# The first steps of a clustered-attention kernel in another order: loads by partition halves, VectorE and GpSimd work moved, and one more maxima row turned on TensorE

## The chip, the cores and the metric

One Trainium2 chip, one of its cores. The metric is the device time of one execution in microseconds (us). Engines are named as in the profile: PE is TensorE (PEld its weight loads), DVE is VectorE, ACT is ScalarE, POOL is GpSimd, SP is SyncE, which only issues DMAs here (SPq in the rows).

## The reference, cut to what matters

Three layers: attention that is masked by clusters, a mixture of eight experts with the best two per token, and a soft mixture. The change lies in the first one.

```python
# q, k, v: 2 batches x 8 heads x 768 x 64; 16 centroids per head
q_assign = np.argmax(np.einsum('bhsd,hcd->bhsc', q_n, c_n), axis=-1)
k_assign = np.argmax(np.einsum('bhsd,hcd->bhsc', k_n, c_n), axis=-1)
mask = q_assign[:, :, :, None] == k_assign[:, :, None, :]
scores = np.where(mask, scale * np.matmul(q, k.transpose(0, 1, 3, 2)), -1000000000.0)
scores = scores - np.max(scores, axis=-1, keepdims=True)
attn = np.exp(scores)
attn = attn / (np.sum(attn, axis=-1, keepdims=True) + 1e-09)
return np.matmul(attn, v)
```

## The kernel before, in words

The 16 heads are worked in 8 pairs. A pair has 12 **steps**: 2 halves of the queries (`qh`) by 6 chunks of 128 keys. The main loop in `body` runs over two steps at a time; pair 0 has steps 0 to 11, pair 1 steps 12 to 23. A **score** (L372 and L374, four products into a `psc` bank) is followed by the exponential on ScalarE (L377, `pt`), and two steps later by `av` (L387, `pav`) on TensorE and the sums of `pt` on GpSimd (L404, L407).

What a pair needs first:

- `load` and `load_s` bring q, k and their stacked form; `sims` multiplies the stacked form with the centroids (L216, `psim`), and DVE turns the result (L219).
- `masks(p, 0..4)` makes one-hot rows of the best cluster: a maximum (L228), an `is_equal` with two SBUF inputs (L230), a transpose (L233), all on DVE; then a product (L237), and two operations on ACT (L238, L241). `mask_rows` carries them into the operands by six DMAs (L281, L285). Pair 0 has its own way: `first_rows` (L250 on PE, L257 on ACT, L261 on DVE).
- `hk`, `hq`, `ak`, `aq` copy the operands on ACT, and `akl`, `aql` make the remainders on POOL (L305, L315), each after the ACT copy it subtracts. POOL also writes constant rows of the operands in `fixed` (L194 to L196).
- The row maxima come ahead of the scores. Per half of the queries there are nine **units** (`munit`): PE multiplies (L333, `pmx`), DVE takes the maximum (L338 and L343, `mp`). Two PSUM banks `mx` take turns, so a unit's product waits for the reduction two units back. `mfin` joins the nine (L348, `nm`) and makes a row of them: for the pairs and halves in `TF` by six small products (L354, `pnm`) and a copy on ACT (L356), for the others by a transpose on DVE (L359, `nmt`) and four DMAs (L362). The scores of that half of the queries need the row.

Every engine does its instructions in the order of the program. That order is written out by hand: before the loop as calls in `body`, and in the loop by the tables `pre` (units, one ahead of each of the two scores, the rest behind them), `mid` (ACT copies) and `post` (everything behind the `av`), with a step for each entry. `U1` and `Z1` set the steps of pair 1's first units and of its first `mfin`, `R1` and `Z0` those of pair 0's second half, `ORD` the mix of `masks(1, ...)` and units ahead of the loop.

`setup2` (L201 to L210) and `Dispatch.setup` (L490 to L516) fill constants for later, nearly all of it on POOL; `Dispatch.setup` has four instructions on DVE, and the first of them (L505, `lim`) waits for POOL (L504). In the kernel before they stand between the first units of pair 0's second half and the loop.

Of the kernel before, what the change touches and what calls it, by code (L numbers as in the profile page):

```python
# [57 lines left out]
B1 = 9  # L58
B7 = 8
B2 = 1  # L60
TF = (0, 0), (0, 1)
RATE = 2, 1, 1, 1, 2, 3, 1, 2, 1, 1, 4, 1, 3
ORD, U1, Z1, R1, Z0 = (1, 1, 1, 0, 1, 0, 1, 1), 3, 8, 4, 2
M2S = 14, 15, 16, 18, 20
MS = 10, 10, 12, 14, 18
G0, GN, KS = 55, 3, 64
# [15 lines left out]
f32 = lambda t: t.bitcast(F32)  # L82


class Attention:
# [6 lines left out]
    def __init__(self, tc, g, qk, q2, k2, v2, cent, wgn):  # L92
        self.tc, self.nc, self.g = tc, tc.nc, g
        self.qk, self.q2, self.k2, self.v2, self.cent, self.wgn = qk, q2, k2, v2, cent, wgn
        at = g.at
        even = g.pre.tile([128, 4, 2 * S], F32R, name="even", tag="pre")
        odda = g.mo1.tile([128, 2, 2 * S], F32R, name="odda", tag="H")
        oddb = at.tile([128, 2, 2 * S], F32R, name="oddb")
        odd = odda[:, 0], odda[:, 1], oddb[:, 0], oddb[:, 1]
        R = lambda k: [t.rearrange("p (h s) -> p h s", h=2) for t in (even[:, k], odd[k])]  # L100
        Q = lambda k: [t.rearrange("p (t h s) -> p t h s", t=2, h=2) for t in (even[:, k], odd[k])]

        self.AK, self.AQ = R(0), Q(1)

        self.BK, self.BQ = R(2), Q(3)
        self.nm = at.tile([128, 32], F32R, name="nm")
        self.raws, self.vt, self.simT, self.mp = {}, {}, {}, {}
        self.ptile, self.stile, self.avp, self.ots, self.rds = {}, {}, {}, {}, {}
        self.u1 = 0

    def busy(self, n):

# [4 lines left out]
    def load(self, p):  # L117
        nc, g = self.nc, self.g
        q, k = g.raw[p % 2][:, 0:2, :], g.raw[p % 2][:, 2:4, :]
        nc.sync.dma_start(q, self.q2[p])  # L120
        nc.sync.dma_start(k, self.k2[p])
        self.raws[p] = (q, k)

    def load_s(self, p):
# [7 lines left out]
    def setup(self):  # L132
# [8 lines left out]

        half = lambda n: g.place(n // 2).bitcast(BF16)

        self.identr = self.AQ[1][:, 1, 1, 256:]
        nc.gpsimd.tensor_copy(self.identr, g.ident)
        self.s16, self.t16, self.first16 = half(384), half(384), half(128)
        self.selk = half(128).rearrange("p (a b c) -> p a b c", a=2, b=2)
# [40 lines left out]
            dv.tensor_scalar(self.selk[:, hh, :, NCL * hh:NCL * hh + NCL],  # L188
                             up[:, 64:128].rearrange("p (t h c) -> p h t c", t=2, h=2)[:, hh], BIG, None, op0=OP.mult)

    def fixed(self):

        nc = self.nc
        nc.gpsimd.memset(f32(self.BK[0])[96:97], 1.0)  # L194
        nc.gpsimd.memset(f32(self.BK[1])[64:96], 0.0)
        nc.gpsimd.memset(f32(self.BK[1])[96:97], 1.0)  # L196

    def setup2(self):
        nc, g, at = self.nc, self.g, self.g.at
# [119 lines left out]
    def munit(self, p, qh, u):  # L319

        nc, g = self.nc, self.g
        i = p % 2
        if u == 0:
            self.mp[p, qh] = g.at.tile([128, 2, 6], F32, name="mp", tag="mp", bufs=2)
        mp = self.mp[p, qh]
        if p or u % 2:
            ps = g.psum.tile([128, 512], F32, tag="mx", bufs=2, name="pmx")
        else:
            ps = g.psum.tile([128, 2, 512], F32, tag="sc", bufs=2, name="pmx")[:, 0]
# [1014 lines left out]
def body(tc, qk, q2, k2, v2, cent, wgn, noise, w12, phi, v12, out):  # L1344
    nc = tc.nc
    with ExitStack() as ctx:
# [43 lines left out]

        g.again = again
        g.stk = M1.WR.rearrange("p a b -> p (a b)")[:, :2 * S].rearrange("p (a s) -> p a s", a=2)
        A = Attention(tc, g, qk, q2, k2, v2, cent, wgn)
        Dp = Dispatch(tc, g, noise)

# [13 lines left out]
        for i in range(2):  # L1409
            A.ak(0, i)  # L1410
            A.akl(0, i)
            if i == 0:
                A.fixed()
        for i in range(2):
            A.aq(0, i)
            A.aql(0, i)
        for u in range(A.MU):
            A.munit(0, 0, u)
        turn = A.sims(1)
# [1 line left out]
        A.busy(B2)  # L1421
        A.mfin(0, 0)
        turn()
        todo1 = [lambda i=i: A.masks(1, i) for i in range(5)] + [lambda: A.mask_rows(1)]
        for i in ORD:
            if i:
                todo1.pop(0)()
            else:
                A.munit(0, 1, A.u1)
                A.u1 += 1  # L1430
        EARLY = A.u1
        A.setup2()
        Dp.setup()

        pre, mid, post = {}, {}, {}

# [3 lines left out]
        for p in range(-1, NP):  # L1440
            s0 = 12 * p
            if p >= 0 and p + 1 < NP:
                n = p + 1
                at(post, s0 + 2, A.load_v, n)
                for s, fn, i in ((0, A.hk, 0), (0, A.hq, 0), (2, A.hk, 1), (2, A.ak, 0), (4, A.ak, 1), (4, A.aq, 0),
                                 (6, A.hq, 1), (6, A.aq, 1)):
                    at(mid, s0 + s, fn, n, i)
                for s, fn, i in ((0, A.akl, 0), (4, A.akl, 1), (6, A.aql, 0), (6, A.aql, 1)):
                    at(post, s0 + s, fn, n, i)
                a, z = (2, 7) if p else (U1, Z1)  # L1450
                for u in range(A.MU):
                    at(pre, s0 + a + 2 * u // 3, A.munit, n, 0, u)
                    at(pre, s0 + 8 + 2 * u // 3, A.munit, n, 1, u)
                at(post, s0 + z, A.mfin, n, 0)
                at(post, s0 + 13, A.mfin, n, 1)
            if p == 0:
                for u in range(EARLY, A.MU):
                    at(pre, (u - EARLY) * 2 // R1, A.munit, 0, 1, u)
                at(post, Z0, A.mfin, 0, 1)
            if p >= 0 and p + 2 < NP:  # L1460
                at(post, s0 + 2, A.load, p + 2)
# [78 lines left out]
        for j in range(2):  # L1540
            at(post, s0 - 4, load_x, j)
            s = s0 + JT[j]
            for i in range(JN):
                at(post, s + i, M1.prep_t, j, i, JN)
                at(post, s + i + JH, M1.prep_h, j, i, JN)
                at(post, s + i + JL, M1.prep_l, j, nc.vector if i % 2 else nc.gpsimd, i, JN)
        end = 12 * NP + 2
        for s0 in range(0, end, 2):
            k = RATE[s0 // 2 - 28] if 56 <= s0 < 82 else 1 if s0 < KS else 3 if s0 < 12 * NP else 0
# [173 lines left out]
```

## Time and profile before

| What | Value |
|---|---|
| median of 3 runs | 644.04 us (643.37 to 644.43) |
| profiled execution | 650.09 us, span 648.3 us |
| mean granted clock of TensorE | 0.981 |
| PE busy | 614.9 us, 95% of the span |
| DVE, ACT, POOL busy | 409.0, 311.3, 289.3 us |

The span is the time from the first to the last instruction; the profiled execution's own time has 1.8 us around it. The profile names the mean length of each group of instructions and, ahead of each, the time the engine sat idle and which engine's event ended it. [...]

### The profile page before, as it was taken

What the parts mean: (1) busy time and instruction counts of PE and PEld (TensorE: products, weight loads), DVE (VectorE), ACT (ScalarE), POOL (GpSimd) and SP (SyncE); (2) the same over time, 40 slices, a digit from 0 to 9 for tenths busy, and PEclk for the clock granted to TensorE, in tenths of its full rate; (3) what the DMA queues carried; (4) which work ended last, traced back from release to release, by engine and by line L of the source; (5) the groups of instructions that cost most, each with busy time, mean ns of one, the idle gap of its engine ahead of it and who ended that gap; (6) DMA issues with size and microseconds to landing.
All of it is one profiled execution on the core that took longest, in us unless ns stands there. A gap on an engine that the chain in (4) does not pass through costs nothing. (4 is left out here: it accounts for less than half of the span.)

```text
span 648.3 us, 11039 instructions
## 1 busy us (share of the span) xinstructions
PE 614.9 (95%) x3967; PEld 472.8 (73%) x3967; DVE 409.0 (63%) x871; ACT 311.3 (48%) x444; POOL 289.3 (45%) x256
## 2 busy tenths in 40 slices
PE   7899999999799999789999999999999999998996
PEld 5567666676566657667888888888888888875544
DVE  6667888778965798566554445554544557645632
ACT  5576585765556582245334334443534445533002
POOL 3899676866758793543124033251423403110100
PEclk8699999999899999989999999999999999999999
DMA  8392845727255713478944829879796868978995
GB/s 317 76 267 79 287 149 179 252 89 275 95 191 167 209 66 131 156 223 232 196 133 110 218 98 272 298 255 258 278 281 234 167 207 276 321 269 271 425 398 198
DMA packets 62890, 139.47 MB, mean 215 GB/s; under 512 B 15280, under 2 KB 30832, under 8 KB 60784
## 3 DMA queue, kind: packets, MB, share of 16 engines
q1 hardware_dynamic: 56944, 125.31, 58.3%
q0 software_dynamic: 5888, 13.42, 9.5%
q8 instruction: 32, 0.52, 0.3%
q14 instruction: 26, 0.21, 0.1%
HBM read 108.18 MB, written 28.42 MB: 211 GB/s over the span
## 5 line engine op out<-in xcount | busy, mean ns | idle before, releaser
L976 PE MATMUL py<-ring,H 128*128 128x512 f32 (+1 forms) x686 | 172.9, 396 | 5.3 <-issue 3.5
L840 DVE TENSOR_TENSOR ring<-wr,ring 128x1024 fp32r<-128x1024 f32 (+1 forms) x77 | 93.5, 1214 | 100.4 <-ACT ring L833 99.5
L976 PEld LDWEIGHTS py<-ring,H 128*128 128x128 f32 (+1 forms) x686 | 123.9, 184 | 32.5 <-issue 3.8
L833 ACT ACTIVATE ring<-wr 128x1024 fp32r<-128x1024 f32 x77 | 81.5, 1059 | 91.7 <-PE py L976 83.6
L377 ACT ACTIVATE pt<-psc 128x768 f32<-128x768 f32 x96 | 77.2, 811 | 71.1 <-PE psc L374 60.8
L984 POOL DMA_INDIRECT x2acc<-y,mdi x31 | 50.2, 1621 | 104.4 <-ACT y L1009 97.6
L387 PE MATMUL pav<-pt,vt 128*64 128x384 f32 x384 | 73.6, 505 | 0.0
L941 ACT ACTIVATE H<-ph 128x256 fp32r<-128x256 f32 (+7 forms) x80 | 36.7, 459 | 75.9 <-PE ph L935 60.9
L338 DVE TENSOR_REDUCE mp<-pmx 128x1 f32<-128x512 f32 x96 | 63.2, 676 | 15.3 <-PE pmx L333 14.4
L935 PE MATMUL ph<-XS1a,ring 128*128 128x240 f32 (+3 forms) x288 | 67.8, 325 | 0.0
L407 POOL TENSOR_TENSOR psa<-psa,pt 128x768 f32<-128x768 f32 x32 | 61.9, 1936 | 4.7 <-ACT pt L377 2.5
L935 PE MATMUL ph<-XS0a,ring 128*128 128x432 f32 (+3 forms) x252 | 63.2, 332 | 0.1
L944 DVE SCALAR_TENSOR_TENSOR H<-ph,H 128x384 fp32r<-128x384 f32 (+2 forms) x120 | 43.4, 389 | 26.3 <-ACT H L941 20.6
L935 PEld LDWEIGHTS ph<-XS1a,ring 128*128 128x128 f32 x288 | 47.7, 188 | 3.6 <-DVE ring L840 0.2
L935 PE MATMUL ph<-XS0b,ring 128*128 128x256 f32 (+3 forms) x192 | 48.2, 325 | 0.8 <-DVE ring L840 0.6
L935 PE MATMUL ph<-XS1b,ring 128*128 128x240 f32 (+3 forms) x192 | 46.1, 313 | 0.8 <-DVE ring L840 0.8
L935 PEld LDWEIGHTS ph<-XS0a,ring 128*128 128x128 f32 x252 | 43.2, 188 | 4.0 <-issue 1.2
L903 POOL TENSOR_TENSOR XS0b<-xr,XS0a 128x512 fp32r<-128x512 f32 (+1 forms) x9 | 17.1, 1901 | 64.5 <-ACT XS0a L897 64.5
L387 PEld LDWEIGHTS pav<-pt,vt 128*64 128x64 f32 x384 | 23.5, 137 | 24.8 <-issue 19.3
L333 PE MATMUL pmx<-even 96*128 96x512 f32 (+1 forms) x96 | 34.0, 415 | 6.2 <-DVE mp L338 4.3
L343 DVE TENSOR_REDUCE mp<-pmx 128x2 f32<-128x512 f32 x48 | 33.0, 689 | 5.5 <-PE pmx L333 5.0
L638 POOL DMA_INDIRECT xg<-x,idx x24 | 25.9, 1077 | 21.1 <-DVE xr L567 14.8
(338 smaller groups left out, 1023.7 us busy)
## 6 DMA issues: line engine op xcount, KB each, us to landing
wr<-in_w SPq DMA_DIRECT2D x80, 512.0 KB
v<-in_v SPq DMA_DIRECT2D x9, 2048.0 KB
xg<-xr SPq DMA_DIRECT2D x14, 512.0 KB
wr<-in_qk SPq DMA_DIRECT2D x8, 768.0 KB
early<-in_q SPq DMA_DIRECT2D x8, 768.0 KB
early<-in_k SPq DMA_DIRECT2D x8, 768.0 KB
x2acc<-xr SPq DMA_DIRECT2D x8, 512.0 KB
vt<-in_v SPq DMA_DIRECT2D x8, 384.0 KB
```

The source lines that it names most:

```text
L333: nc.tensor.matmul(o, self.BQ[i][:96, qh, hh, 128 * c:128 * c + 128], self.BK[i][:96, hh, ks], start=True, stop=True)
L338: nc.vector.tensor_reduce(mp[:, 0, col:col + 1], ps, axis=AX.X, op=OP.max)
L377: nc.scalar.activation(pt, ps[:, :, :384], AF.Exp, scale=SCALE)
L387: nc.tensor.matmul(self.avp[p, qh][64 * hh:64 * hh + 64, :384], self.vt[p][:, hh, kc, :], pt[:, hh, :], start=(kc == 0), stop=(kc == 5))
L407: eng.tensor_tensor(s, s, pt.pop((p, t)), op=OP.add)
L833: self.nc.scalar.activation(self.ring[s][0], self.wr[s], AF.Copy)
L840: nc.vector.tensor_tensor(lo[:, :n], wr[:, :n], f32(hi)[:, :n], op=OP.subtract)
L935: nc.tensor.matmul(ph[:, :u], a[:, 128 * c:128 * c + 128], x[:, c, :u], start=(c == 0 and i == 0), stop=(c == 3 and i == 2))
L941: nc.scalar.activation(HH[:, :u], ph[:, :u], AF.Relu)
L944: nc.vector.scalar_tensor_tensor(o[:, :b - a], ph[:, a:b], 0.0, f32(HH)[:, a:b], op0=OP.max, op1=OP.subtract)
L976: nc.tensor.matmul(o, x, y, start=(f == 0 and i == 0), stop=(f == NF - 1 and i == 2))
L984: st = nc.gpsimd.indirect_dma_start(out=out, out_offset=bass.IndirectOffsetOnAxis(ap=di, axis=0), in_=y, in_offset=None, compute_op=OP.add)
```

## The change

Four edits. The loads of pair 0 are cut into partitions 0 to 63 and 64 to 127, k ahead of q. `fixed` is cut in two calls, the part for pair 1 behind the last `aql` of pair 0. Ahead of the loop `masks(1, 0..2)` now stand together in front of two units (both in `mx` banks), three filler products follow (`busy(B3)`), and `masks(1, 3)`, `masks(1, 4)`, `mask_rows(1)` and the other seven units move behind or between the first scores; `setup2` and `Dispatch.setup` move into the loop, behind the first remainder of pair 1. The units of pair 1 get later steps (4 and 10 in place of 3 and 8), and its first row is turned on PE at step 9 in place of four DMAs at step 8; its second row comes at step 15 in place of 13.

```diff
-TF = (0, 0), (0, 1)
+B3, EARLY = 3, 2
+TF = (0, 0), (0, 1), (1, 0)
-ORD, U1, Z1, R1, Z0 = (1, 1, 1, 0, 1, 0, 1, 1), 3, 8, 4, 2
+FIRST, R1, Z0 = (4, 9, 10, 15), 3, 3
     def load(self, p):
-        nc.sync.dma_start(q, self.q2[p])
-        nc.sync.dma_start(k, self.k2[p])
+        for r in (slice(0, 64), slice(64, 128)) if p == 0 else (slice(0, 128),):
+            for t, src in ((k, self.k2), (q, self.q2)) if p == 0 else ((q, self.q2), (k, self.k2)):
+                nc.sync.dma_start(t[r], src[p, r])
-        self.identr = self.AQ[1][:, 1, 1, 256:]
+        self.identr = g.turner
-    def fixed(self):
+    def fixed(self, i):
-        nc.gpsimd.memset(f32(self.BK[0])[96:97], 1.0)
-        nc.gpsimd.memset(f32(self.BK[1])[64:96], 0.0)
-        nc.gpsimd.memset(f32(self.BK[1])[96:97], 1.0)
+        if i:
+            nc.gpsimd.memset(f32(self.BK[1])[64:96], 0.0)
+        nc.gpsimd.memset(f32(self.BK[i])[96:97], 1.0)
-        if p or u % 2:
+        if p or qh or u % 2:
...
             A.akl(0, i)
-            if i == 0:
-                A.fixed()
+        A.fixed(0)
         for i in range(2):
             A.aq(0, i)
             A.aql(0, i)
+        A.fixed(1)
...
-        todo1 = [lambda i=i: A.masks(1, i) for i in range(5)] + [lambda: A.mask_rows(1)]
-        for i in ORD:
-            if i:
-                todo1.pop(0)()
-            else:
-                A.munit(0, 1, A.u1)
-                A.u1 += 1
-        EARLY = A.u1
-        A.setup2()
-        Dp.setup()
+        for i in range(3):
+            A.masks(1, i)
+        for u in range(EARLY):
+            A.munit(0, 1, u)
+        A.busy(B3)
...
-                a, z = (2, 7) if p else (U1, Z1)
+                a, z, a1, z1 = (2, 7, 8, 13) if p else FIRST
+                for i in range(0 if p else 2):
+                    at(pre, s0 + a, lambda: None)
                 for u in range(A.MU):
                     at(pre, s0 + a + 2 * u // 3, A.munit, n, 0, u)
-                    at(pre, s0 + 8 + 2 * u // 3, A.munit, n, 1, u)
+                    at(pre, s0 + a1 + 2 * u // 3, A.munit, n, 1, u)
                 at(post, s0 + z, A.mfin, n, 0)
-                at(post, s0 + 13, A.mfin, n, 1)
+                at(post, s0 + z1, A.mfin, n, 1)
             if p == 0:
+                for fn in (0, 0, lambda: A.masks(1, 3), lambda: A.masks(1, 4), lambda: A.mask_rows(1)):
+                    at(pre, 0, fn or (lambda: None))
                 for u in range(EARLY, A.MU):
-                    at(pre, (u - EARLY) * 2 // R1, A.munit, 0, 1, u)
+                    at(pre, 0 if u < EARLY + R1 else 2, A.munit, 0, 1, u)
...
+        at(post, 0, A.setup2)
+        at(post, 0, Dp.setup)
```

`g.turner` is a room of a later layer's tile (`XS1a`), free until then, for the identity that turns the rows.

The order on POOL at the start, from the first remainder to the constants, before:

```order
L305 TENSOR_TENSOR even<-early,even 64x768 [waits DMAHW3_49,Activation_49]
L194 MEMSET even 1x1536 [waits Pool_49]
L195 MEMSET oddb 32x1536
L196 MEMSET oddb 1x1536
L305 TENSOR_TENSOR even<-early,even 64x768 [waits Activation_49]
L315 TENSOR_TENSOR even<-early,even 64x768 [waits DMAHW2_49,Pool_49]
L315 TENSOR_TENSOR even<-early,even 64x768 [waits Activation_49]
L201 MEMSET iw 128x4x32 [waits Pool_49]
```

and now:

```order
L306 TENSOR_TENSOR even<-early,even 64x768 [waits DMAHW2_49,Activation_49]
L306 TENSOR_TENSOR even<-early,even 64x768 [waits Activation_49]
L197 MEMSET even 1x1536 [waits Pool_49]
L316 TENSOR_TENSOR even<-early,even 64x768 [waits DMAHW3_49,Pool_49]
L316 TENSOR_TENSOR even<-early,even 64x768 [waits Activation_49]
L196 MEMSET oddb 32x1536
L197 MEMSET oddb 1x1536 [waits Pool_49]
L306 TENSOR_TENSOR odda<-early,oddb 64x768 [waits DMAHW1_49,Activation_49]
L202 MEMSET iw 128x4x32 [waits Pool_49]
```

Between the last constant row (`oddb`) and `setup2` (`iw`) now stands a remainder of pair 1 (`odda`), which waits for ACT. On DVE, the same place before, from `masks(1, 0)` on (`mp` is a unit's reduction, a row with x2 is two of them):

```order
L228 TENSOR_REDUCE xr<-xr 128x24 [waits DVE_49]
L230 TENSOR_TENSOR xr<-xr 128x384 [waits DVE_49]
L233 STREAM_TRANSPOSE xr<-xr 128x384 [waits DVE_49]
L338 TENSOR_REDUCE mp<-pmx 128x1 [waits PE_49] x2
L505 TENSOR_SCALAR lim<-lim 128x2 [waits Pool_49]
L513 TENSOR_SCALAR tri<-ident_i 128x128
```

and now:

```order
L234 STREAM_TRANSPOSE xr<-xr 128x384 [waits DVE_49]
L339 TENSOR_REDUCE mp<-pmx 128x1 [waits PE_49] x2
L344 TENSOR_REDUCE mp<-pmx 128x2 [waits PE_49]
L339 TENSOR_REDUCE mp<-pmx 128x1 [waits PE_49] x2
L220 STREAM_TRANSPOSE xr<-psim 128x384 [waits PE_49]
L506 TENSOR_SCALAR lim<-lim 128x2 [waits Pool_49]
L514 TENSOR_SCALAR tri<-ident_i 128x128
```

The wait for POOL stood behind two units of pair 0's second half and now stands behind five of them and the turn of pair 2's `psim`; the last four units are behind it. On PE, behind the `av` of steps 6 and 7, before:

```order
L333 MATMUL pmx<-oddb 128x256 x4
L387 MATMUL pav<-pt,vt 64x384 x4
L216 MATMUL psim<-wr,xr 32x384 x4
L333 MATMUL pmx<-oddb 128x512
L372 MATMUL psc<-even 128x384
```

and now:

```order
L334 MATMUL pmx<-oddb 128x256 x2
L388 MATMUL pav<-pt,vt 64x384 x4
L217 MATMUL psim<-wr,xr 32x384 x4
L355 MATMUL pnm<-XS1a,nm 1x128 x6
L334 MATMUL pmx<-oddb 128x512
L373 MATMUL psc<-even 128x384
```

The turn of pair 1's first row (`pnm`) comes right behind `psim`, and one unit fewer stands ahead. On PE again, in the pair of steps 14 and 15, before, from the score of step 15 on:

```order
L374 MATMUL psc<-odda 128x384
L333 MATMUL pmx<-even 128x256 x2
L387 MATMUL pav<-pt,vt 64x384 x4
L237 LDWEIGHTS xr
L237 MATMUL pfst<-xr 128x384
```

and now:

```order
L375 MATMUL psc<-odda 128x384
L334 MATMUL pmx<-even 128x512 x2
L334 MATMUL pmx<-oddb 128x256 x2
L334 MATMUL pmx<-even 128x256 x2
L388 MATMUL pav<-pt,vt 64x384 x4
```

Here one unit stood behind the second score, and now four do.

## Rows read from the trace of the kernel before

**Rows 1.** Part 1 of the page: busy us (share of the span) xinstructions of each engine

```profile
PE 614.9 (95%) x3967; PEld 472.8 (73%) x3967; DVE 409.0 (63%) x871; ACT 311.3 (48%) x444; POOL 289.3 (45%) x256
```

**Rows 2.** Windows of 10 us: length, busy per engine, PEclk, DMA share, GB/s

```profile
20.00:30.00 10.00, 7.36 (x26) 4.51 (x27) 6.24 (x13) 4.63 (x7) 9.18 (x44) 0.63 0.33 105
40.00:50.00 10.00, 10.00 (x59) 6.76 (x59) 6.19 (x11) 6.84 (x12) 9.61 (x7) 1.00 0.85 328
```

**Rows 3.** A window of 1 us in the first loads, same columns

```profile
5.00:6.00 1.00, 0.79 (x4) 0.43 (x3) 0.50 (x3) 0.07 (x1) 0.00 (x0) 1.00 1.03 424
```

**Rows 4.** Timeline at the start: start us, length us, instruction, [idle before <-releaser]

```profile
8.50 0.56 DVE L230 TENSOR_TENSOR xr<-xr 128x384 bf16<-128x384 f32 x1
9.64 0.84 ACT L294 ACTIVATE even<-early 64x768 fp32r<-64x768 f32 x1 [4.56 <-DMA early<-in_k]
10.40 0.95 DVE L261 TENSOR_SCALAR even<-pmq 32x768 fp32r<-32x768 f32 x1 [0.74 <-PE pmq L250]
10.56 1.81 POOL L305 TENSOR_TENSOR even<-early,even 64x768 fp32r<-64x768 f32 x1 [8.63 <-ACT even L294]
...
12.09 0.95 PE L333 MATMUL pmx<-even 96*128 96x512 f32 x2 [1.24 <-ACT even L257]
```

**Rows 5.** Timeline, the longest `is_equal`, beside a POOL sum

```profile
52.27 1.60 DVE L230 TENSOR_TENSOR xr<-xr 128x384 bf16<-128x384 f32 x1
```

**Rows 6.** Timeline from the first row's copy to the wait for POOL

```profile
19.64 0.80 ACT L356 ACTIVATE even<-pnm 1x768 fp32r<-1x768 f32 x1 [0.21 <-PE pnm L354]
...
21.93 0.49 ACT L238 ACTIVATE xr<-pfst 128x384 f32<-128x384 f32 x1 [1.49 <-PE pfst L237]
...
22.45 0.61 ACT L241 ACTIVATE xr<-xr,al 64x384 f32<-64x384 f32 x1
...
22.61 0.21 POOL L201 MEMSET iw<- 128x128 f32 x1
...
25.53 0.69 DVE L505 TENSOR_SCALAR lim<-lim 128x2 f32<-128x2 f32 x1 [2.67 <-POOL lim L504]
...
25.89 0.68 DVE L343 TENSOR_REDUCE mp<-pmx 128x2 f32<-128x512 f32 x1
```

**Rows 7.** Timeline from pair 0's second maxima to the second `av`

```profile
35.55 0.15 DVE L348 TENSOR_REDUCE nm<-mp 128x6 fp32r<-128x12 f32 x1
...
35.85 0.52 PE L354 MATMUL pnm<-odda,nm 128*1 128x128 f32 x6 [0.70 <-DVE nm L348]
...
36.51 0.35 PE L372 MATMUL psc<-even 97*128 97x384 f32 x1
...
37.23 0.39 PE L333 MATMUL pmx<-oddb 96*128 96x512 f32 x1
...
37.42 0.81 ACT L377 ACTIVATE pt<-psc 128x768 f32<-128x768 f32 x1 [0.21 <-PE psc L374]
...
38.49 1.51 PE L387 MATMUL pav<-pt,vt 128*64 128x384 f32 x8
```

**Rows 8.** Timeline behind the scores of steps 8 and 9

```profile
46.42 1.51 PE L387 MATMUL pav<-pt,vt 128*64 128x384 f32 x8
...
47.87 0.85 PE L216 MATMUL psim<-wr,xr 128*32 128x384 f32 x8
48.65 0.50 PE L333 MATMUL pmx<-oddb 96*128 96x512 f32 x1
...
48.79 0.58 DVE L219 STREAM_TRANSPOSE xr<-psim 128x384 f32<-128x384 f32 x1 [0.98 <-PE psim L216]
```

**Rows 9.** Timeline behind the scores of steps 14 and 15

```profile
59.11 1.25 DVE L338 TENSOR_REDUCE mp<-pmx 128x1 f32<-128x512 f32 x2
59.22 2.95 SPq L362 DMA_DIRECT2D oddb<-nmt  x4
...
59.81 0.30 PEld L333 LDWEIGHTS pmx<-even 96*128 96x128 f32 x2 [0.20 <-DVE mp L338]
...
60.25 1.51 PE L387 MATMUL pav<-pt,vt 128*64 128x384 f32 x8
```

More of the change, by code (lines that the diff above doesn't have):

```diff
@@ L108, in __init__ @@
         self.ptile, self.stile, self.avp, self.ots, self.rds = {}, {}, {}, {}, {}
-        self.u1 = 0
     def busy(self, n):
@@ L1392, in body @@
         g.stk = M1.WR.rearrange("p a b -> p (a b)")[:, :2 * S].rearrange("p (a s) -> p a s", a=2)
+        g.turner = M1.XT[1][0][:, :128]
         A = Attention(tc, g, qk, q2, k2, v2, cent, wgn)
```

## The prediction

> **What bounds the kernel now.** I read the page's busy shares first, then the windows, then the timeline of the first 65 us. TensorE (PE) is busy for 95% of the span [rows 1]. [...] The timeline names the waits of the start: PE's first unit waits for ACT at 12.09, and ACT for the loads until 9.64 [rows 4]; at 25.53 DVE has idled 2.67 us for POOL, which fills constants from 22.61 on, and the units queue behind it [rows 6]; at 35.85 PE waits 0.70 us for the second maxima of pair 0 [rows 7].
>
> **The change, part by part.** I take the profiled execution's own times and follow the one chain that the new order sets.
>
> *Loads by halves.* ACT's first copy reads k, partitions 0 to 63. Behind that half now come three others of 393 KB; at the 424 GB/s of the window [rows 3] they take 2.78 us, so the copy starts at 9.64 - 2.78 = 6.86 in place of 9.64 and ends 0.84 later, at 7.70 [rows 4]. But POOL's remainder follows that copy by 0.08 us and runs 1.81 us [rows 4], now from 7.78 to 9.59, and DVE's `is_equal` is due at 8.50. That operation takes 0.56 us with POOL idle [rows 4] and 1.60 us when it starts beside a running POOL sum [rows 5]. I let it wait for POOL's end and finish 0.42 later, at 10.01 in place of 9.06: 0.95 us late. DVE's first query rows move from 10.40 to 11.35, end at 12.30, and PE's first unit starts at 12.35 in place of 12.09 [rows 4]. So the split costs 0.26 us and gains nothing; without that meeting the first unit would wait for DVE's rows at 11.35 and start at 11.40, 0.69 earlier. These two values are the bounds; I take the late one.
>
> *Up to the copy of the first row.* Nine units and their reductions are as before, so the copy on ACT starts at 19.64 + 0.26 = 19.90 and ends at 20.70 [rows 6]. `fixed`, cut in two on POOL, costs nothing: POOL is ahead of ACT there and comes to wait anyway (below). The three filler products lie beside that copy; I cost them at nothing.
>
> *The first scores.* They no longer wait for units, so score 0 starts at 20.75, and its exponential 0.91 later (36.51 to 37.42 in [rows 7]), at 21.66. In the new order ACT then does two exponentials (0.81 each), the two operations of the masks (0.49 and 0.61 [rows 6]) and pair 1's first copy (0.84), with small gaps: 23.3, 24.4, 25.3. Only then can POOL make pair 1's first remainder (1.81): 27.1. And the constants stand behind that remainder now. From `iw` at 22.61 to DVE's `lim` at 25.53 they took 2.92 us [rows 6], so `lim` comes at 30.0, and the reduction behind it ends 1.04 later (25.53 to 26.57): 31.05. DVE has by then reduced five units and turned `psim`, and idles some 4 to 5 us in place of 2.67. PE does scores 0 to 3 early, up to unit 6, and then stands, because unit 7 needs the bank of unit 5, whose reduction is behind `lim`. This is the heart of the forecast: the scores gain, and DVE's wait takes the gain.
>
> *From 31.05 to the second `av`.* Three more reductions of 0.68 bring DVE to 33.1; now the first two mask operations of pair 2 stand ahead of `mfin` (the maximum, which I take as long as a free `is_equal`, 0.56, and `is_equal` itself with 0.56 to 1.60 [rows 4, 5]; I take 1.1), so the second maxima are ready at 35.0 in place of 35.70, and PE's turn starts at 35.2 in place of 35.85 [rows 7]. PE needs it no earlier: unit 8 and the first `av`, 1.51 at the high clock and 3.0 at the low one, begin at about 32.3. Behind the turn come score 4 and, after the turn's 0.52 and the row's copy of 0.80 [rows 6, 7], score 5 at 36.6. A score's products take 0.72 (36.51 to 37.23 [rows 7]). Then three units of pair 1 follow in one go: the third waits for the first one's reduction, 1.2 us behind the first, and the `av` comes 0.45 later: 36.6 + 0.72 + 1.65 = 39.0, against 38.49 [rows 7]. Loss: 0.5 us, from -0.1 to 1.4 by the two ends of `is_equal` and of the clock.
>
> *Steps 8 and 9.* The row that left by four DMAs now holds PE. `psim` starts at 47.87 and is turned on DVE from 48.79 for 0.58; `mfin` follows (0.15), and PE's six products 0.15 behind that, at 49.7. They occupy PE for some 0.4, so the next unit starts at 50.1 in place of 48.65 [rows 7, 8]: 1.4 us. One unit fewer ahead gives 0.25 back. Loss: 1.15 us.
>
> *Steps 14 and 15.* The three units that were put off arrive here, beside pair 2's three. In this place PE already waits for the reductions (its weight load 0.20 at 59.81 [rows 9]), so the three cost DVE's pace of 0.65 each (1.25 for two [rows 9]): 1.95 us. If PE hid a little of it, 1.5; I take 1.9. Most of this is work that earlier steps no longer do, and those steps' saving is counted above.
>
> *The second row of pair 1* leaves two steps later, by four DMAs that take 2.95 us to issue [rows 9], behind the loads of pair 3 on the queue, with one pair of steps (some 4 us: two pairs from 38.49 to 46.42 [rows 7, 8]) left. By the rows it lands about when it is wanted. I take nothing, with 1.0 as the upper end.
>
> **Sum:** 0.5 + 1.15 + 1.9 = 3.55 us slower. The profiled execution would take 650.09 + 3.55 = 653.6; it stands 6.05 above the median of the runs shown, 644.04, and nothing says that the terms scale with that, so the forecast is 644.04 + 3.55 = **647.6 us**. Its own range: 646.0 (no meeting at `is_equal`, the short masks, 1.5 for the units) to 650.2 (the other ends and the late row).
>
> **Rivals.** *1. The scores' gain is kept* (faster). If POOL's constants were done in time, DVE would reduce unit 5 right behind `psim`, at about 26.4 in place of 31.05; the whole stretch up to the second `av` would come 4.6 earlier, and the sum is 3.55 - 4.65 = -1.1, or 642.9; with the short ends of the other terms, 641.5. The place is POOL's queue ahead of `iw`, and each us by which `lim` comes ahead of 30.0 is worth one: it decides at `lim` = 26.5. For it speaks that POOL's recorded lengths are the least certain of the trace; against it that ACT's four operations ahead of pair 1's copy alone take 2.7 us.
>
> *2. The later steps don't pay.* If steps 8 and 14 find slack on PE that the windows hide (pipelined products can look busy while they wait), their 3.05 us shrink to 0.5: 644.04 + 1.0 = 645.0, no change. For it speaks that weight loads fill only two thirds of those windows [rows 2]; against it the 0.20 of idle time in front of the very units.
>
> [...]
>
> **How the numbers follow.** A measurement can tell some 0.2%, or 1.3 us, from no change. My forecast has 0.60, rival 3 0.12, rival 2 0.14, rival 1 0.14. The predicted time is that of the forecast, 647.6. From rival 2's 645.0 upward lies 0.86; to hold 8 in 10 the range goes a little under it, 643.8, and up to 650.2, where the unknown costs end. Faster by over 0.2% is rival 1 with its 0.14 less a part that ends nearer: 0.13. No change is rival 2 and that part: 0.15. Slower is the rest, 0.72.
>
> **What would show it.** Right: DVE idles over 3.5 us in front of `lim`, with POOL's first remainder of pair 1 starting after 24 us; PE idles over 3 us between 25 and 31; the second `av` no earlier than 38.4; about 1 us of idle time ahead of the six small products behind `psim`; the wait of PE for reductions in steps 14 and 15 grown to about 1 us. `is_equal` at 8.5 of about 1.5 us shows the meeting with POOL. Wrong: `lim` before 27 us, or PE at work through the twenties; then the scores' gain was kept, and the time is under 644.

## The result, and the profile after

The changed kernel took 651.36 us (median of 5, 649.92 to 653.72) beside 644.43 us of the kernel before on the same chip: ratio 1.0103, interval 1.007 to 1.0136. A second set of runs gave 1.0097 (1.0077 to 1.0116). That is between 6 and 7 us slower. The forecast was 3.55 us slower, at most 6.2, so the sign was right and the size was not; the measured time lies 1.2 us above the range.

The profiled execution took 653.72 us, span 651.9. Busy shares first, then the two windows that answer to [rows 2] (third number from the end: TensorE's granted clock, 1.00 is full speed; its low level is 0.50, as in before from 23 to 32 us):

```profile
PE 617.4 (95%) x3979; PEld 474.0 (73%) x3979; DVE 412.6 (63%) x870; ACT 312.1 (48%) x445; POOL 287.8 (44%) x256
```

```profile
20.00:30.00 10.00, 9.35 (x52) 7.38 (x48) 6.30 (x12) 6.74 (x11) 6.21 (x6) 0.80 0.27 93
40.00:50.00 10.00, 9.41 (x49) 6.55 (x49) 5.92 (x9) 7.84 (x12) 9.47 (x7) 1.00 0.96 297
```

The shares tell nothing: PE is at 95% in both. The twenties look better than before (9.35 us of work in place of 7.36, the scores have come forward), the forties worse (9.41 in place of 10.00). The timeline from the first copy to the second `av`, with the lines that answer to [rows 4, 6, 7]:

```profile
8.53 0.84 ACT L295 ACTIVATE even<-early 64x768 fp32r<-64x768 f32 x1 [3.47 <-DMA early<-in_k]
9.46 1.83 POOL L306 TENSOR_TENSOR even<-early,even 64x768 fp32r<-64x768 f32 x1 [7.54 <-ACT even L295]
9.53 2.18 DVE L231 TENSOR_TENSOR xr<-xr 128x384 bf16<-128x384 f32 x1
...
14.16 0.70 PE L334 MATMUL pmx<-even 96*128 96x512 f32 x2 [0.65 <-DVE even L262]
...
21.53 0.80 ACT L357 ACTIVATE even<-pnm 1x768 fp32r<-1x768 f32 x1 [0.44 <-PE pnm L355]
...
22.25 1.48 PE L115 MATMUL pb<-ident 128*128 128x128 f32 x6
...
23.39 0.67 PE L373 MATMUL psc<-even 97*128 97x384 f32 x1
...
28.03 1.85 POOL L306 TENSOR_TENSOR odda<-early,oddb 64x768 fp32r<-64x768 f32 x1 [3.74 <-ACT oddb L295]
...
32.72 0.69 DVE L506 TENSOR_SCALAR lim<-lim 128x2 f32<-128x2 f32 x1 [4.24 <-POOL lim L505]
...
33.82 1.39 PE L334 MATMUL pmx<-even 96*128 96x512 f32 x3 [3.91 <-DVE mp L344]
...
35.15 2.77 PE L388 MATMUL pav<-pt,vt 128*64 128x384 f32 x8
...
36.44 1.97 DVE L231 TENSOR_TENSOR xr<-xr 128x384 bf16<-128x384 f32 x1
...
42.48 1.51 PE L388 MATMUL pav<-pt,vt 128*64 128x384 f32 x8
```

The chain is the one of the forecast, link by link, and late. `is_equal` meets POOL's remainder and takes 2.18 us; the first unit starts at 14.16 (before 12.09); DVE idles 4.24 us for `lim`; PE stands 3.91 us behind it; the second `av` comes at 42.48 (before 38.49). Behind the scores of steps 8 and 9, and of steps 14 and 15, to set beside [rows 8, 9]:

```profile
50.07 1.51 PE L388 MATMUL pav<-pt,vt 128*64 128x384 f32 x8
...
53.21 0.52 PE L355 MATMUL pnm<-XS1a,nm 128*1 128x128 f32 x6 [0.84 <-DVE nm L349]
...
55.83 1.51 PE L388 MATMUL pav<-pt,vt 128*64 128x384 f32 x8
...
65.48 0.30 PEld L334 LDWEIGHTS pmx<-oddb 96*128 96x128 f32 x2 [0.65 <-DVE mp L339]
...
66.51 1.51 PE L388 MATMUL pav<-pt,vt 128*64 128x384 f32 x8
```

From 50.07 to 55.83 are 5.76 us (before 4.55), and the `av` in the pair of steps 14 and 15 is 6.26 us late. From there PE has no slack: the **second px** (six products, the first mark behind everything that was moved) starts at 76.04 (before 69.78), and each px after it is 6.25 to 6.28 us late until 157 us. I use it as the yardstick of the runs below. The two spans differ by 3.6 us only, because the profile of before lost some 3.6 us more by the ranking of the second layer: its permutation is made at 285.5 us, and at 281.5 in the run e1 below, which is 0.4 us ahead at the second px. What that loss is was not tried.

### The profile page after: what moved, and what is told of

Its sections match the earlier page's. It is cut to its first block, busy times and chain, and to the rows that moved or that the text cites. A ratio compares the mean times of both kernels' runs of the same rounds, so it can differ in the third digit from the quotient of the medians.

```text
span 651.9 us, 11055 instructions
## 1 busy us (share of the span) xinstructions
PE 617.4 (95%) x3979; PEld 474.0 (73%) x3979; DVE 412.6 (63%) x870; ACT 312.1 (48%) x445; POOL 287.8 (44%) x256
## 5 line engine op out<-in xcount | busy, mean ns | idle before, releaser
L388 PE MATMUL pav<-pt,vt 128*64 128x384 f32 x384 | 75.1, 514 | 0.0
L936 PE MATMUL ph<-XS0b,ring 128*128 128x256 f32 (+3 forms) x192 | 46.6, 316 | 1.5 <-ACT ring L834 0.9
L334 PE MATMUL pmx<-oddb 96*128 96x512 f32 (+1 forms) x96 | 32.1, 377 | 3.8 <-DVE mp L339 3.5
```

What stands on the lines that cost most here:

```text
L334: nc.tensor.matmul(o, self.BQ[i][:96, qh, hh, 128 * c:128 * c + 128], self.BK[i][:96, hh, ks], start=True, stop=True)
L388: nc.tensor.matmul(self.avp[p, qh][64 * hh:64 * hh + 64, :384], self.vt[p][:, hh, kc, :], pt[:, hh, :], start=(kc == 0), stop=(kc == 5))
L936: nc.tensor.matmul(ph[:, :u], a[:, 128 * c:128 * c + 128], x[:, c, :u], start=(c == 0 and i == 0), stop=(c == 3 and i == 2))
```

## The experiments

All runs, with the ratio to the kernel before on the same chip, and the second `av` and second px of the one profiled execution (us). Beside the rows marked * the kernel before took 650.4 or 653.2 us in place of 644 to 646, so only ratios are compared there. The kernel before run against itself gave 1.0015: less than that tells nothing.

| Run | Ratio (interval) | second av | second px |
|---|---|---|---|
| before, first profile | | 38.49 | 69.78 |
| r2, before again* | 1.0015 (0.9995 to 1.0036) | 37.75 | 69.48 |
| changed, first profile | 1.0103 (1.0070 to 1.0136) | 42.48 | 76.04 |
| r1, changed again | 1.0097 (1.0077 to 1.0116) | 40.29 | 73.81 |
| e1, before + split loads | 1.0005 (0.9990 to 1.0020) | 38.49 | 69.41 |
| e2, whole loads | 1.0087 (1.0064 to 1.0109) | 41.57 | 76.48 |
| e3, loads by heads | 1.0076 (1.0056 to 1.0095) | 41.38 | 74.94 |
| e4, late remainder | 1.0086 (1.0066 to 1.0106) | 40.21 | 73.77 |
| e5, early constants | 1.0061 (1.0035 to 1.0086) | 36.60 | 70.14 |
| e6, old steps | 1.0044 (1.0027 to 1.0062) | 39.63 | 70.89 |
| e7, no fillers | 1.0114 (1.0082 to 1.0146) | 40.65 | 75.46 |
| e8, filled hole | 1.0096 (1.0078 to 1.0114) | 38.74 | 73.12 |
| e9, late DVE* | 1.0120 (1.0083 to 1.0156) | 36.44 | 78.44 |
| e10, late DVE and DMAs* | 0.9969 (0.9946 to 0.9992) | 36.71 | 71.05 |
| c1 | 1.0091 (1.0061 to 1.0122) | 45.01 | 76.28 |
| c2 | 1.0072 (1.0045 to 1.0099) | 35.02 | 73.18 |
| c3 | 0.9983 (0.9967 to 0.9999) | 36.36 | 68.20 |
| c4* | 1.0024 (0.9998 to 1.0049) | 33.17 | 69.82 |
| c5* | 0.9972 (0.9945 to 1.0000) | 34.29 | 66.70 |
| c6* | 0.9948 (0.9914 to 0.9981) | 34.78 | 66.60 |

### Is it the loads? (e1 to e4)

My first theory was that the split is the missing loss: the first unit 2.07 us late, from half loads at half the rate (203 GB/s against 409, below) and from the meeting. e1 is before with the new `load`; e2 is the changed kernel with the old one; e3 and e4:

```diff
 e3
+        for hh in (0, 1) if p == 0 else (slice(0, 2),):
...
+                nc.sync.dma_start(t[:, hh], src[p][:, hh])
 e4
         for i in range(2):
             A.ak(0, i)
-            A.akl(0, i)
+        for i in (1, 0):
+            A.akl(0, i)
```

> The kernel before with the split loads alone. Theory H (the halves load at about half the rate, 203 to 221 GB/s in the changed kernel's windows from 6 to 12 us against 412 to 430 before, and POOL's first remainder then falls on DVE's is_equal): the first unit comes at about 14.2 us in place of 12.09, is_equal takes over 2 us in place of 0.56, and the time grows by 1.5 to 2.5 us, to about 646.4. Rival R (the split is neutral, as my forecast had it, and the loss sits in the new order behind it): first unit within 0.4 us of 12.09, time within 0.5 us of 644.4.

> The changed kernel with the whole loads of before. H: first unit at 12.1 in place of 14.16, second av at 40.4 in place of 42.48, time 649.3 (651.4 less 2.1), which leaves some 5 us of loss for the rest of the change. R: first unit moves, but the second av stays near 42.5 and the time at 651.4, because DVE's wait for POOL decides.

> The changed kernel with the four first loads cut by heads: as many transfers of as many bytes, k ahead of q, but each on all 128 partitions. H (it is the 64 partitions): the windows from 6 to 12 us show over 380 GB/s in place of 203 to 221, ACT's first copy starts before 7.5 us in place of 8.53, and the time falls by about 2 us, to 649.3; the remainder then meets is_equal as I forecast, at about 1.5 us. Rival (four transfers are dear by their number): 203 to 221 GB/s again and 651.4.

> The changed kernel, with POOL's two first remainders in the other order, so that the one that ran beside is_equal waits for an ACT copy that ends at 14.6 us. If the meeting is the dearer part of H: is_equal takes 0.56 us in place of 2.18, the first products of the masks come at 10.8 in place of 12.38, the first unit at 12.6 to 13.2 in place of 14.16, and the time falls by 1.0 to 1.6 us, to about 650. If the halves' rate alone is (late psim, late copies): is_equal stays over 1.5 us, or the first unit waits for ACT instead, and the time stays at 651.4.

The theory does not carry the loss. e2, e3 and e4, each without the half loads or without the meeting, still lose 0.8 to 0.9%, against 1.0% with both; the 0.1 to 0.3% between them are what the theory had forecast for e3, but the intervals overlap. And e1 met the remainder as badly as the changed kernel, and had lost nothing at the second `av` or in the time; the timeline of e1:

```profile
10.04 2.20 DVE L231 TENSOR_TENSOR xr<-xr 128x384 bf16<-128x384 f32 x1
...
14.69 0.70 PE L334 MATMUL pmx<-even 96*128 96x512 f32 x2 [0.65 <-DVE even L262]
...
25.01 0.69 DVE L506 TENSOR_SCALAR lim<-lim 128x2 f32<-128x2 f32 x1
...
33.65 1.51 PE L388 MATMUL pav<-pt,vt 128*64 128x384 f32 x8
```

2.6 us late at the first unit, 0.01 late at the first `av` (before 33.64). Two things closed the gap. DVE's wait for POOL took in a part of it: POOL's constants were not late, so `lim` comes at 25.01 without idle time, where before it comes at 25.53 behind 2.67 us of it, and `psim` of pair 2 starts 1.48 us late (29.26, before 27.78). The clock took in the rest: in the window of 30 to 32 us the granted clock is 0.79 in e1 and 0.50 in before; it went back to the high level 2 us earlier. And e2, whose chain ran 2.46 us ahead of the first profile's at the second maxima (35.87 against 38.33), gave it back in a long low stretch: a granted clock of 0.57 from 30 to 36 us and 0.50 from 36 to 44.

The rate was measured, though. The window of 6 to 7 us, in the changed kernel and then in e3, which has as many transfers of as many bytes on all 128 partitions:

```profile
6.00:7.00 1.00, 0.24 (x4) 0.23 (x8) 0.78 (x6) 0.00 (x0) 0.00 (x0) 1.00 0.94 203
```

```profile
6.00:7.00 1.00, 0.57 (x8) 0.19 (x8) 0.78 (x6) 0.00 (x0) 0.00 (x0) 1.00 1.05 409
```

Halves move 203 GB/s where heads move 409 (last column), and ACT's first copy starts at 8.53 and 7.01. In e4 `is_equal` took 0.56 us, but so it did in e5 to e8, which have the changed kernel's order there: with the half loads and that order the meeting comes only where pair 0's `psim` takes 1.51 us in place of 0.85 (four profiles of ten: the first, e1, e9, e10). What makes it take longer there is not shown.

### The changed kernel and the kernel before, a second time (r1, r2)

> The changed kernel a second time, for another profiled execution. If its first profile met a start that most executions don't have (psim of 1.51 us in place of 0.85, so that is_equal started behind POOL's remainder and took 2.18): psim 0.85, is_equal 0.56, first unit at 11.9 to 12.4, first score at 20.2 to 21.6, lim on POOL at about 29 to 30, the hole of 3.9 us in TensorE's work still there, second px between 73.5 and 76.5 by the granted clock behind the hole. Rival: is_equal takes 2.2 us again and the first unit comes at 14.

> The kernel before a second time, for another profiled execution. If its first profile (650.09 us) lost its extra time behind 250 us, in the ranking of the second layer: second px at 69.4 to 69.8 again, the last product some 4 us earlier than 635.3, and a time near 646. Rival (the start differs from execution to execution as it does with the changed kernel): second px over 0.7 us away from 69.78.

The timeline of r1:

```profile
8.42 0.84 ACT L295 ACTIVATE even<-early 64x768 fp32r<-64x768 f32 x1 [3.35 <-DMA early<-in_k]
8.75 0.56 DVE L231 TENSOR_TENSOR xr<-xr 128x384 bf16<-128x384 f32 x1
9.35 1.81 POOL L306 TENSOR_TENSOR even<-early,even 64x768 fp32r<-64x768 f32 x1 [7.42 <-ACT even L295]
...
11.85 0.73 PE L334 MATMUL pmx<-even 96*128 96x512 f32 x2 [0.73 <-ACT even L258]
...
19.97 1.48 PE L115 MATMUL pb<-ident 128*128 128x128 f32 x6
...
21.10 0.67 PE L373 MATMUL psc<-even 97*128 97x384 f32 x1
...
30.54 0.69 DVE L506 TENSOR_SCALAR lim<-lim 128x2 f32<-128x2 f32 x1 [4.24 <-POOL lim L505]
...
31.64 1.39 PE L334 MATMUL pmx<-even 96*128 96x512 f32 x3 [3.91 <-DVE mp L344]
...
32.96 2.83 PE L388 MATMUL pav<-pt,vt 128*64 128x384 f32 x8
...
34.25 1.97 DVE L231 TENSOR_TENSOR xr<-xr 128x384 bf16<-128x384 f32 x1
...
40.29 1.51 PE L388 MATMUL pav<-pt,vt 128*64 128x384 f32 x8
```

So the start has two forms. Here `is_equal` starts first, runs free, and the first unit is 0.24 us earlier than before; in the first profile it started 0.07 us behind POOL's remainder. Between these two profiles that is 2.2 us at the second px (76.04, 73.81). r2's start is that of before within 0.3 us at the second px; its last product came at 636.8, later than expected, on a chip where all runs were longer.

### The hole and what lies behind it (e7, e8, e5, c2, e9, e10)

e7 sets `B3 = 0`. e8 puts 14 filler products in the place where PE waits:

```diff
                 for u in range(EARLY, A.MU):
+                    if u == 7:
+                        at(pre, 2, A.busy, 14)
```

> The changed kernel without the three filler products ahead of the first score. If they delay score 0 (it starts 1.06 us behind the end of the row's copy): score 0 at 22.4 in place of 23.39, and the chain through ACT, POOL's remainder and lim 1.0 us earlier, time 650.4. Rival (they keep TensorE busy so that its clock rises at 24 us): without them the granted clock stays at 0.5 past 24 us, and nothing is gained.

> The changed kernel with 14 filler products (0.256 us each at the high clock, 3.6 us) on TensorE in the place where it waits for DVE's reduction behind lim; nothing else waits for them. If the idle hole is what brings the granted clock down to 0.5 behind it: the clock stays at 1.00 from 30 to 40 us, the first av takes 1.51 us in place of 2.77, the second av comes 1 to 3 us earlier, and the time falls by 1 to 3 us, to about 649. Rival (the clock falls by itself, or the low stretch costs nothing because DVE and POOL set the pace): first av still near 2.8 us, or the second av unmoved; time 651.4.

Without the fillers score 0 came at 20.32 and `lim` at 29.34, 1.2 us ahead of r1, and nothing was gained at the second px or in the time: the granted clock was 0.50 from 30 to 43 us. It had been 1.00 from 20 to 29 us, so the rival's reason doesn't hold either. With the hole filled, the window of 32 to 34 us (r1, then e8):

```profile
32.00:34.00 2.00, 1.90 (x7) 1.03 (x8) 1.79 (x4) 0.00 (x0) 1.93 (x3) 0.56 0.47 26
```

```profile
32.00:34.00 2.00, 1.90 (x11) 0.78 (x10) 2.00 (x4) 0.00 (x0) 2.00 (x5) 1.00 0.34 15
```

The clock stays at 1.00 and the second `av` comes 1.55 us earlier than in r1, as expected; but the second px gains 0.69 and the time nothing that can be told. The rest of the 1.55 went again behind a later `is_equal`, which took 2.03 us in place of 0.88. With the idle time went the low clock (1.00 in place of 0.56 in this window), and a low stretch as short as r1's (3.4 us) is a small part of the price: 0.7 of 4.0 us at the second px.

e5 moves `setup2` and `Dispatch.setup` ahead of the loop, without the four DVE operations; c2 does so too but leaves the DMAs of the constants in the loop (the expectations count five; there are four). e9 moves the four DVE operations alone, and e10 those DMAs with them:

```diff
 e9
         at(post, 0, A.setup2)
         at(post, 0, Dp.setup)
+        at(post, 5, Dp.setup_dve)
 e10
+        at(post, 5, A.setup2_dma)
```

> The changed kernel with POOL's constants back ahead of the loop, in front of pair 1's first remainder; the four DVE operations that use them stay where they are. If the wait for POOL carries the loss: lim on POOL at about 27 us in place of 32.47, DVE's 4.24 us of idle time gone, second maxima near 34.1 in place of 38.33, second av near 38.3 in place of 42.48, px of the second half near 71.8 in place of 76.04, time 647.2. Rival (TensorE's low clock takes back what the wait gives, as it did with the whole loads): the wait goes, but the granted clock is 0.5 for longer between 30 and 40 us, and the time is 650 or more.

> The changed kernel with POOL's constants ahead of the loop, as in the run with early constants, but their five DMAs left where the change has them, behind the mask rows on the queue. That run lost 0.84 us and more at pair 1's first unit, which waited for the mask rows behind those DMAs. If the queue was the rest of the loss: no wait for the mask rows ahead of pair 1's first unit, second av near 35.3, second px near 69, time about 645. Rival (nothing left to gain): second px near 70.1 and a time near 650, as with the early constants.

> The changed kernel with only its four DVE operations on POOL's constants moved, from the first pair of steps to step 5; POOL's order and the DMA queue stay as they are. If DVE's wait for lim is the cause of the hole: the reduction of the sixth unit follows psim's turn, TensorE's hole of 3.9 us at 28 to 32 us is gone or under 1 us, the first av takes 1.51 us, the second av comes at about 36 in place of 40.3 (the second profile of the changed kernel), the second px at 69.5 to 71 in place of 73.8, time 647 to 648. Rival (POOL's late remainder or the queue holds the chain anyway): the wait is gone but the second av stays behind 39 and the time at 651 or more.

> As the run that moved DVE's four operations to step 5, with the five DMAs of the constants moved there as well, behind the loads of v, q, k and of pair 3's stacked operand on SP's queue. In that run psim of pair 3 waited 5.14 us for its operand (issued at 37.54, behind the constants' DMAs; psim at 50.68), and gave back all that the missing wait had gained. If the queue was that second bound: the operand's load is issued 2.5 to 4 us earlier, psim follows the av of steps 6 and 7 without a wait, the second px comes at 69.5 to 71.5 in place of 73.8 (78.4 in that run), and the time is 0.3 to 0.5% above the kernel before, in place of 1.0%. Rival (the load itself is slow, whatever its place): psim still waits over 2 us, and the time stays 1% above.

This settled it. In e9 the hole is gone and the second `av` comes at 36.44, 6 us ahead of the first profile, which had the same start; then this (e9: issues on SP's queue, the constants' four DMAs first, and what waits for the last one shown; then e10):

```profile
30.98 1.36 SPq L206 DMA_DIRECT2D iw<-in_wgn  x2
32.39 0.60 SPq L493 DMA_DIRECT2D noise<-in_noise  x1
34.12 0.41 SPq L512 DMA_DIRECT2D xg<-xr  x1
34.57 1.92 SPq L130 DMA_DIRECT2D vt<-in_v  x1
...
37.54 0.91 SPq L126 DMA_DIRECT2D wr<-in_qk  x1
...
50.68 1.50 PE L217 MATMUL psim<-wr,xr 128*32 128x384 f32 x8 [5.14 <-DMA wr<-in_qk]
```

```profile
31.28 0.58 SPq L130 DMA_DIRECT2D vt<-in_v  x1
...
32.93 0.38 SPq L126 DMA_DIRECT2D wr<-in_qk  x1
...
45.74 0.85 PE L220 MATMUL psim<-wr,xr 128*32 128x384 f32 x8
```

`psim` of pair 3 stood 5.14 us for its operand, whose load is issued behind the constants' DMAs. These hold the queue from 30.98 to 34.57: for 1.4 us of that they wait for POOL, the rest is their own issue, and the load of v behind them takes 1.92 us to issue in place of 0.58. With them out of the way the operand's load is issued 4.6 us earlier, `psim` doesn't wait, and the second px comes 7.4 us earlier (71.05 against 78.44) with the same bad start. That is more than 5.14: e9's granted clock is 0.50 from 48 to 58 us as well, and its `psim` takes 1.50 us in place of 0.85.

e10 is the changed kernel with nothing but these eight instructions elsewhere, and it is faster than the kernel before (0.9969, interval under 1), where 0.3 to 0.5% slower was expected. So the loss is in the place of these eight instructions. Where e10 gains on the kernel before is not shown: in its profile, the longest of its 12 executions, the second px is still 1.3 to 1.6 us later, and the kernel before was not profiled on that chip. e10 is no plain undoing either, since the kernel before has the four DMAs ahead of the same loads.

e5 and c2 lost part of their gain in the same queue: in e5 pair 1's first unit waited 0.84 us for the mask rows, in c2 `psim` stood 3.13 us for that load. e5's executions spread from 645.5 to 652.6 us, and the profiled one (646.8) is among the five shortest of twelve, so its marks flatter it.

### The steps of pair 1 (e6)

```diff
-TF = (0, 0), (0, 1), (1, 0)
+TF = (0, 0), (0, 1)
-FIRST, R1, Z0 = (4, 9, 10, 15), 3, 3
+FIRST, R1, Z0 = (3, 8, 8, 13), 3, 3
```

> The changed kernel with pair 1's units, maxima and row at the steps and by the DMAs of before. If steps 8, 9, 14 and 15 cost what the trace shows (from the second av to the second px 33.56 us in place of 31.29): that stretch is 31.3 again, the second px near 73.8 in place of 76.04, time 649.1. Rival: the units that come earlier again fall into the stretch up to the second av and cost there what they save later; the second px stays near 76 and the time at 651.4.

From the second `av` to the second px it took 31.26 us, as in before (31.29) and 2.3 us less than in r1 (33.52). The ratio fell from 1.0097 to 1.0044, some 3.4 us; the rest of that is not in this stretch.

### Versions ahead of both (c1, c3 to c6)

c1 joins e3, e4, e5 and e6. c3 joins e3, e4, e6 and c2. c4 joins e3, e4, e6 and e9; c5 is c3 with the four DVE operations and two of the DMAs at step 5, and c6 has the other two DMAs there too.

> The changed kernel with four things undone or mended at once: loads cut by heads, the first two remainders on POOL in the other order, the constants ahead of the loop, pair 1's steps and DMAs as before. If the four costs are apart and add (2.3 of the meeting, 4.2 of the wait, 2.3 of the steps): second px near 67.3, that is 2.5 us ahead of the kernel before (69.78), and the time near 642. Rival (TensorE's clock sets the stretch to 34 us whatever the order is): second px within 1 us of 69.78 and the time of before.

> The same, with the loads cut by heads, POOL's two first remainders in the other order, and pair 1's steps and DMAs as before. If the costs add (2.3 us of the steps on top): second px near 67, time 642 to 643, ahead of the kernel before. Rival (pair 1's units, at the earlier step, come ahead of the mask rows and wait for them, or the low clock takes the gain): second px no better than 69.5, time 645 or more.

> The four DVE operations at step 5, pair 1's steps and DMAs as before, the loads cut by heads and POOL's first remainders in the other order; scores first, as in the change. If the costs add: no hole, second px near 67.5, time 643 to 644, ahead of the kernel before. Rival (the mask rows of pair 1 come too late for units at the earlier step): PE waits for them ahead of pair 1's first unit, second px 69 or more, time 645 or more.

> As the last run but with POOL's constants ahead of the loop too, that is the run that beat the kernel before with its four DVE operations and DMAs at step 5. If the rest of the hole (2.3 us for lim at 27.3) was still worth its length there: second px near 66.5 in place of 68.2, time 643. Rival (the mask rows or TensorE's clock set that stretch): second px 68 again and the time 645.

> The best kernel so far (scores first, POOL's constants ahead of the loop, DVE's four operations at step 5, pair 1's steps as before, loads by heads) with the last two DMAs of the constants at step 5 too. If the order of the queue still costs there: second px at or under 66.5 (66.7 in that run, 69.5 in the kernel before), time 0.3 to 0.5% below the kernel before. Rival: second px above 67 or a time within 0.2% of the kernel before.

c1 was a miss that pointed to the queue (its timeline):

```profile
37.54 1.19 PE L334 MATMUL pmx<-oddb 96*128 96x512 f32 x2 [7.85 <-DMA oddb<-xr]
```

Its mask rows were issued behind the constants' DMAs, and a unit at the old, earlier step waited 7.85 us for them. c4 stood 4.18 us at the same `psim` as e9, c3 still 0.86 us, with 2.58 us of DVE's wait for `lim` left; c5 and c6 stand at neither. c6 is 0.5% faster than the kernel before (0.2 to 0.9%), with the second px at 66.60.

## Why the prediction was wrong

Step by step, in its own numbers (us):

| Step | forecast | first profile | r1 |
|---|---|---|---|
| first unit | 12.35 | 14.16 | 11.85 |
| copy of the first row | 19.90 | 21.53 | 19.25 |
| score 0 | 20.75 | 23.39 | 21.10 |
| `lim` on DVE | 30.0 | 32.72 | 30.54 |
| second maxima | 35.0 | 38.33 | 36.15 |
| second `av` | 39.0 | 42.48 | 40.29 |
| loss up to there (0.5) | +0.5 | +3.99 | +1.80 |
| steps 8 and 9 | +1.15 | +1.21 | +1.20 |
| steps 14 and 15 | +1.9 | +1.73 | +1.74 |
| second px | +3.55 | +6.26 | +4.03 |

**Right:** the mechanism, DVE's wait for `lim` behind pair 1's remainder, with PE standing for 3.91 us (from 27.7 in r1, from 29.9 in the first profile), and what that does to the scores' gain. Steps 8, 9, 14 and 15 were right to 0.2 us each; what the rows give beyond (-0.7), and the sum left out, is the unit fewer in two other pairs of steps. e6 shows the same cost from the other side. The signs that were to show it right are in the trace, but for `is_equal`: 2.18 or 0.56 us, never 1.5. Rival 2 fell with steps 8 and 14; products do overlap in the records (384 of `pav` in 73.6 us of busy time, at a mean of 505 ns each, on the page of before), but no slack came of it there. That a loss is carried on in full, as the sum has it, holds from the second px to 157 us (6.25 to 6.28 us at each px); ahead of that a loss of 2.6 us could vanish (e1).

**The step that failed** is the first term of the sum, up to the second `av`: 0.5 us, from -0.1 to 1.4, measured 1.80 and 3.99. Three things were mis-sized in it. The meeting of `is_equal` and POOL was taken into the sum with 0.95 us; it comes in some executions only, and then makes the first unit 2.3 us and the second px 2.2 us later (first profile against r1), because the halves load at half the rate (203 GB/s from 6 to 7 us, where 424 were taken) and POOL starts at 9.4, not at 7.8. That they land late was rival 3, with a chance of 0.12; no row of before has a load of 64 partitions, and no rival had both orders of the start in one kernel. The three fillers were costed at nothing; at the low clock, in both profiles (0.50 from 20 to 24 us in the first; the fillers take 1.48 us in both), score 0 starts 1.05 us behind the end of the copy (20.05, 21.10 in r1), and in e6, with the clock at 1.00 there, 0.14 us. Whether that delay is paid at the end is not shown, as e7 gained nothing without them. The second `is_equal` was taken as 1.1 us and bounded by 1.60; beside POOL's sums it took 1.97 in both, and from `lim` to the second maxima it is 5.61 us in place of 5.0. The first `av` lay within its bounds (1.51 us at the high clock, 3.0 at the low one): 2.77 and 2.83, at a granted clock of 0.50 for all but its last 0.2 us.

With these the second px is 4.0 us late in r1 and 6.3 in the first profile, where the sum had 3.55: an average near 5, by four profiles in ten with the meeting. The measured 6.3 to 6.9 are a little more: r1 lost another 1.6 us behind 286 us against e1. Stretches there differ between executions by as much, and what they hold was not tried, so between one and two us of the loss stay open.

The range is not the sum of the ends that it names either: these give 645.6 (-0.1 + 1.15 + 1.5, less 0.95 for the meeting) and 649.5 (1.4 + 1.15 + 1.9 + 1.0), not 646.0 and 650.2. The measured time lies above both.

**Rival 1** had the price nearly right, though its condition didn't come (`lim` at 30.54 and 32.72, not by 26.5), and it was incomplete. It priced `lim` in time at 4.65 us; e9 and the first profile, with equal starts, lie 6.0 us apart at the `av` behind the scores of steps 8 and 9 (44.03 against 50.07). But it named POOL's queue as the only place. `setup2` and `Dispatch.setup` also have four DMAs on SP's queue, and the prediction counted POOL's instructions and DVE's and not these. They stand ahead of the loads of v, q, k and pair 3's operand, in the kernel before as well; the change made all of them later. Pair 1's mask rows, which come first on that queue, are issued from 24.45 in r1 (before 22.49), and the last of the four waits 0.8 us for POOL. The operand's load, before:

```profile
32.92 0.39 SPq L125 DMA_DIRECT2D wr<-in_qk  x1
```

and in r1, with the `psim` that needs it:

```profile
35.46 0.73 SPq L126 DMA_DIRECT2D wr<-in_qk  x1
...
49.32 0.85 PE L217 MATMUL psim<-wr,xr 128*32 128x384 f32 x8
```

In the four runs where `psim` waited for this load (e9, c2, c3, c4) it took 12.6 to 13.1 us from its issue. By that it would land at 48.1 to 48.6 in r1, as an estimate, about 1 us ahead of `psim`. So the wait for `lim` hid a second one of nearly the same length, and a fix of the first alone showed little (c2) or nothing (e9).

## What to carry to other kernels

Of a block that is moved, follow its DMAs down their queue as well as its instructions down their engine: transfers that wait for a producer, or only take long to issue, hold back every load issued behind them (here four of them held it for 3.6 us, and a load behind was issued 4.6 us later), and the one who stands for that load is found far down the trace (here 13 us). Where one wait is removed and the time doesn't move, look at the next wait for the same engine before giving the first one up; two chains of equal length look like a wrong theory. Take two profiles of a kernel whose start can fall in two ways before a difference of 2 us is explained.

## What the runs showed of the hardware that I had not expected

- Loads of 64 partitions moved 203 to 221 GB/s in every window of 1 us from 6 to 12 us of the first profile, though all four transfers were issued by 4.23 us; the same bytes on 128 partitions moved 409 in the window of 6 to 7 us (e3), and the whole loads of before 412 there: half the rate for the halves of 393 KB. What halves it is not shown.
- In the meeting of DVE and POOL, DVE's operation was the one that grew (2.18 us, 0.56 without it). Where `is_equal` started 0.07 us behind POOL's remainder, it ended 0.42 us after POOL's end (9.46 + 1.83 = 11.29; 9.53 + 2.18 = 11.71), and POOL's 1.83 us were not lengthened. In e3 the second number is 0.42 again. In r1 `is_equal` took 0.56 us and was over 0.04 us before the remainder began (1.81), so no run here shows the meeting with `is_equal` first.
- The granted clock fell from 1.00 to 0.50 at the hole in each of the seven profiles that have one of 3.9 us. In four of them (the first, r1, e3, e4) it fell when PE had been at work again for 0.2 to 0.6 us, and stayed low for 3.4 us; in e2, e6 and e7 it fell while PE still stood, and stayed low for 6.8 us (e6) or some 13.7 (e2, e7). Filled with products, the same stretch stayed at 1.00 (e8, 28 to 36 us). A start that was 2.6 us late could cost nothing (e1), because a wait for POOL took in some 1 us of it and the clock had risen 2 us earlier.
